# Banded attention feeding a two-layer MLP on one core: V's way to the windows, the mask and the first batch rearranged

## The chip, the cores and the metric

The kernel runs on one core of a Trainium2 chip. The metric is device time in microseconds, from the first to the last instruction of the program, as the median of several runs. The engines of the core are TensorE (PE in the profile, with its weight loads as PEld), VectorE (DVE), ScalarE (ACT), GpSimd (POOL) and SyncE (SP). SyncE and ScalarE start transfers through hardware queues, GpSimd through a software queue; all of them share 16 DMA engines.

## The reference

Eight batches with eight heads each, 576 positions, head size 64. Each position looks at itself and the 63 positions before it. The output of attention, 4608 rows of 512, goes through a two-layer network with 2048 hidden units.

```python
batch, n_heads, seq, head_dim = (8, 8, 576, 64)
n_tokens, d_model, d_ff = (4608, 512, 2048)

scores = np.matmul(q, k.transpose(0, 1, 3, 2)) / np.sqrt(D)
rel = pos[:, None] - pos[None, :]
mask = (rel >= 0) & (rel < 64)
attn = softmax(np.where(mask, scores, -1e9))
x = (attn @ v).transpose(0, 2, 1, 3).reshape(B * S, H * D)
h = x @ w_in
g = h - np.tanh(h)
return g @ w_out
```

## The kernel before

**Attention.** The 576 positions of a batch are nine windows of 64 queries. A window of queries sees 128 keys: its own 64 and the 64 before. Heads are worked in pairs (NP = 4 pairs in a batch, 32 pairs in all, numbered g). For a pair the kernel needs kT and qT (head dimension on the partitions), computes scores with keys on the partitions, takes the exponential on ScalarE into PT, and multiplies PT with the V window `vw[b % 2]`, which holds for each window j the 128 keys on its partitions, all heads, and a column of ones that gives the denominators. `norm` divides on VectorE and writes xs, with queries on the partitions. xs is then turned to xT (features on the partitions): by `x_tr`, transposes on TensorE that are copied out of PSUM by two engines, or by `x_dma`, DMA transposes on SyncE's queue (L346).

**V.** `load_v` or `load_v_all` brings V through GpSimd's queue, which casts from float32 to bf16, to 72 partitions with eight positions each. `cast_v` rearranges it to `vb`, where a position has all its heads side by side. `keys_v` sends 64 keys from eight partitions of vb to the upper half of one window, one transfer for each of the nine windows. The lower half of window j + 1 is the upper half of window j: `shift_v` copies it, as one DMA of 64 partitions (L176) or as copies on VectorE (L174). The shift waits for all nine transfers that it reads. Lower and upper half of each window are in place only then. vb exists once, so the casts of the next batch wait for the transfers that read it.

**The mask.** Batches 0 and 1 (pairs 0 to 7) go through `tile_scores` and `tile_pv`, where an additional product with `hide` pushes forbidden scores far down. Pairs from 8 on go through `scores`, `masking` and `pv`; their mask is made on GpSimd as `seen` and turned by TensorE into PSUM (`make_mask`).

**The network.** Nine chunks of 512 tokens (c = 0 to 8). For each chunk 16 steps "h" (four products with w_in, L361, then tanh on ScalarE, L366, and a subtraction on VectorE, L373) and 16 steps "y" (four products with w_out, L385; after four such steps a copy on ScalarE to one of three ysb buffers and an output transfer on SyncE's queue).

**Order.** Everything is ordered by hand. Before the first step stands batch 0: loads, products that only keep TensorE busy (`warm`, L238), casts, transposes of k and q for a pair (`tr_heads`), scores, PV, norms and turns. Then come 320 numbered steps h; `OPS` says which product stands at which step: chunk 0's h at the even steps 0 to 30, its y at 32 to 47, chunk 1's h at 48 to 63, its y at 64 to 79, chunk 2's h at 80 to 95, and from step 96 on h of chunk c at the even steps and y of chunk c - 1 at the odd ones. `at(h, ...)` hangs attention work behind the product of step h. Each engine works through its own queue in the order in which the program emits it, so an instruction that waits holds all behind it on that engine. `std` hangs the parts of one pair: casts, transposes (`tr`, bank 3), scores (bank 4), masking, PV and norm. In the loop over pairs from 12 on, a is the step of a pair's first transpose, cv the step of a V cast, ky that of the V transfers, sh that of the shift. GpSimd holds back some loads by `pace`, a one-element copy that waits for a certain step of the network.

The lines of the steps that matter most in the version before:

```python
at(36, lambda: [cast_v(1, pr, V) for pr in range(NP)])
at(37, lambda: [keys_v(1, j, G) for j in range(NJ)])
at(38, make_mask)
at(49, lambda: [keys_v(2, j, G) for j in range(NJ)])
at(58, shift_v, 2, 0, NJ - 1, Y)
```

Of the kernel before, what the change touches and what calls it, by code (L numbers as in the profile page):

```python
# [15 lines left out]
def kernel(  # L16
# [27 lines left out]
    qk_pool = ctx.enter_context(tc.tile_pool(name="qk", bufs=3))  # L44
# [36 lines left out]
    def move(eng, o, i):  # L81
        if eng is nc.scalar:
            nc.scalar.activation(o, i, ACT.Copy)  # L83
        else:
            eng.tensor_copy(o, i)  # L85

    def load(g, n, eng):

        b, pr = divmod(g, NP)
        if eng is nc.gpsimd:  # L90
            if (b, n) not in whole:
                whole[b, n] = all_pool.tile([P, H, E * D], BF16, tag=n, name=n + "all")
            t = whole[b, n][:, pr::NP]
        else:
            t = qk_pool.tile([P, 2, E * D], F32, tag="f", name=n + "f")
        eng.dma_start(out=t, in_=(q if n == "q" else k)[b, pr::NP].rearrange("h (p e) d -> p h (e d)", e=E))
        stage[g, n] = t
# [18 lines left out]

    def cast_flat(g, n, eng):
        t = row_pool.tile([P, E, 2, D], BF16, tag=n + "b", name=n + "b").rearrange("p e h d -> p (e h d)")
        t = t.rearrange("p (h c) -> p h c", h=2)
        move(eng, t, stage.pop((g, n)))  # L120
        stage[g, n] = t
# [27 lines left out]
    def load_v(b, pr):  # L149
        if (b, "v") not in whole:  # L150
            whole[b, "v"] = v_pool.tile([PV, H, EV * D], BF16, tag="v", name="vall")
        t = whole[b, "v"][:, pr::NP]
        nc.gpsimd.dma_start(out=t, in_=v[b, pr::NP].rearrange("h (p e) d -> p h (e d)", e=EV))
        stage[b, pr, "v"] = t

    def load_v_all(b):
        t = v_pool.tile([PV, H, EV * D], BF16, tag="v", name="vall")
        nc.gpsimd.dma_start(out=t, in_=v[b].rearrange("h (p e) d -> p h (e d)", e=EV))
        for pr in range(NP):
            stage[b, pr, "v"] = t[:, pr::NP]  # L160

# [41 lines left out]

    nc.vector.memset(ident, 0.0)
    nc.vector.memset(hide, 0.0)
    nc.vector.memset(qT[0], 0.0)
    for i in range(2):
        nc.vector.memset(kT[i][:, 0:64], 0.0)
    nc.vector.memset(vb[:, :, :, D], 1.0)
# [8 lines left out]

    def make_mask():
        nc.gpsimd.memset(seen, 1.0)  # L220
        nc.gpsimd.affine_select(seen, seen, compare_op=ALU.is_ge, fill=0.0,
                                base=-1, pattern=[[1, 128]], channel_multiplier=-1)
        nc.gpsimd.affine_select(seen, seen, compare_op=ALU.is_ge, fill=0.0,
                                base=64, pattern=[[-1, 128]], channel_multiplier=1)
        nc.tensor.transpose(mask, seen, ident[0:64, 0:64])
# [9 lines left out]
    def warm(n):  # L235

        for _ in range(n):
            nc.tensor.matmul(ps[:, 7, :], qT[0][:, 0, 0:128], qT[0][:, 0, 0:512], start=True, stop=True)  # L238

    def tr_heads(g, which, bank, eng):  # L240

        src = stage.pop((g, which))
        tp = ps[:, bank, :].bitcast(BF16)[:, 0:E * P].rearrange("c (e p) -> c e p", e=E)
        for e in range(E):
            for h in range(2):
                nc.tensor.transpose(tp[64 * h:64 * h + 64, e, :], src[:, h, D * e:D * e + D], ident[:P, :P])  # L246
        o = qs[g % 2] if which == "q" else kT[g % NR][:, 64:]
        move(eng, o.rearrange("c (p e) -> c p e", e=E), tp.rearrange("c e p -> c p e"))
# [103 lines left out]
    gT = {}  # L352
# [55 lines left out]
    def at(h, fn, *args):  # L408
        items.setdefault(h, []).append((fn, args))
# [12 lines left out]
    load(0, "q", Y)  # L422
    load(0, "k", A)
    for pr in range(NP):
        load_v(0, pr)
# [4 lines left out]
    for g in 2, 3:  # L430
        load(g, "k", G)
        load(g, "q", G)

    warm(8)
    cast_flat(0, "q", V)
    cast_flat(0, "k", A)
    tr_heads(0, "k", 2, V)
    tr_heads(0, "q", 3, A)
    for pr in range(NP):
        cast_v(0, pr, V)  # L440
    tile_scores(0, 0, (0, 1))
    tile_scores(0, 1, (4, 5))
    for j, eng in enumerate((Y, G, A, Y, G, G, A, Y, G)):
        keys_v(0, j, eng)
    load_w_in(0)
    load_w_in(1)
    for g, eq in (1, A), (2, V), (3, V):
        tr_heads(g, "k", 2, V)
        tr_heads(g, "q", 3, eq)
        tile_scores(g, 0, (0, 1))  # L450
        tile_scores(g, 1, (4, 5))
# [6 lines left out]
    load(7, "k", G)  # L458
    shift_dve(0, 0, 4)
    tile_pv(0, (6, 7))  # L460
    tile_pv(1, (2, 3))
    x_tr(0, 0, 0, 4, 4, A)
    tile_pv(2, (6, 7))
    x_tr(0, 0, 4, 9, 5, A)
    warm(3)
    tile_pv(3, (2, 3))
    warm(3)
# [3 lines left out]
    at(34, more_constants)  # L471
    at(36, lambda: [cast_v(1, pr, V) for pr in range(NP)])
    at(37, lambda: [keys_v(1, j, G) for j in range(NJ)])
    at(37, load, 7, "q", G)
    at(37, load_v_all, 2)
    for g in 8, 9:
        at(37, load, g, "k", G)
        at(37, load, g, "q", G)
    at(38, make_mask)
# [3 lines left out]
    at(41, tr_heads, 5, "k", 3, V)  # L483
    at(42, tr_heads, 5, "q", 0, A)
    at(42, tile_scores, 4, 1, (4, 5))
    at(43, tile_scores, 5, 0, (4, 5))
    at(43, tr_heads, 6, "k", 3, V)
    at(44, tr_heads, 6, "q", 0, A)
    at(44, tile_scores, 5, 1, (4, 5))
    at(45, tile_scores, 6, 0, (4, 5))  # L490
    at(45, shift_dve, 1, 0, 4)
    at(46, tr_heads, 7, "k", 3, V)
    at(46, tr_heads, 7, "q", 0, A)
    at(46, tile_scores, 6, 1, (4, 5))
# [12 lines left out]
    at(49, lambda: [keys_v(2, j, G) for j in range(NJ)])  # L507
# [3 lines left out]
    at(58, shift_v, 2, 0, NJ - 1, Y)  # L511
# [30 lines left out]
    for g in range(3 * NP, B * NP):  # L542
# [3 lines left out]
        cv, ky, sh = s - 72 + 5 * pr, s - 54, s - 47  # L546
        if b == 3:
            a = (65, 71, 76, 81)[pr]
            cv, ky, sh = 63 + pr, 67, 73
        elif b == 4:  # L550
            a = 84 + 7 * pr
            cv, ky, sh = 74 + 3 * pr, 86, 92
        elif b == 5:
            cv, ky, sh = 95 + 4 * pr, 110, 116
        at(cv, cast_v, b, pr)
        if b == 3:
            std(g, a - 1, a - 2, a, a + 2, a + 3, a + 8, a + 11)
            if pr == 0:
                for j in range(NJ):
                    at(ky + j // 2, keys_v, b, j)  # L560
                at(sh, shift_v, b, 0, NJ - 1)
            if pr == NP - 1:
                at(a + 12, x_dma, b)
            continue
# [22 lines left out]
        for j in range(NJ):  # L587
            if pr == 0:
                at(ky + j // 2, keys_v, b, j)
        if pr == 0:  # L590
            if b > 3:
                hq, hk = s - (60 if b < 7 else 68), s - (64 if b < 7 else 72)
                hv = {4: 69, 5: 92}.get(b, s - 78)
                if b == 4:
                    hq, hk = 72, 71
                for h, f in (hv, (load_v_all, b)), (hq, (load_all, b, "q")), (hk, (load_all, b, "k")):
                    at(h, pace, h)
                    at(h, *f)
            at(sh, shift_v, b, 0, NJ - 1)
# [52 lines left out]
```

## Time and profile before

| | |
|---|---|
| median of 3 runs | 391.17 us |
| lowest, highest | 386.18, 395.22 us |
| span of the profiled run | 389.9 us |
| mean granted TensorE clock | 0.950 |
| TensorE busy | 335.6 us, 86% |
| VectorE busy | 197.7 us, 51% |
| ScalarE busy | 182.1 us, 47% |
| GpSimd busy | 115.8 us, 30% |
| first product of chunk 0 | at 31.1 us |

The page divides the span into 40 slices of 9.75 us; each digit is the busy share of a slice in tenths. In the row of TensorE, 9 is full and a low digit is a gap:

```profile
PE   7869938978887699259969999999699999999996
DVE  4345801358834568407853766666266644344310
PEclk9999976999999899759996999999899999999999
DMA  9999768569398132991367759945971130101012
```

TensorE has two deep gaps, in the sixth slice (48.8 to 58.5 us) and in slice 17 and 18 (156 to 175 us). The granted clock is lower in and behind them. A group of instructions is listed with its busy time, the mean duration of one, and the idle time of its engine before it, with what ended that idle time. The two groups of the network's products on TensorE are the two largest:

```profile
L361 PE MATMUL ps<-xT,wi 128*128 128x512 bf16 x576 | 147.2, 384 | 15.6 <-DMA xT<-xs 10.4
L385 PE MATMUL ps<-w_out_sb,gT 128*128 128x512 bf16 x576 | 148.7, 389 | 0.0
```

### The profile page before, as it was taken

To read this page: it belongs to the slowest core of one execution; us is meant where nothing else is said; L and a number is where in the kernel's file an instruction comes from. 1 tells how busy PE (TensorE), PEld (TensorE's weight loads), DVE (VectorE), ACT (ScalarE), POOL (GpSimd) and SP (SyncE) were. 2 spreads that over 40 slices of the span, in tenths; PEclk is the share of its full clock that TensorE was granted. 3 is DMA by queue.
4 is the path that set the end of the run, shared out by engine and by line. 5 is a ranking of instruction groups with operands and counts; after the bars stand their busy time and mean duration, and the time that the engine had idled before them with its cause. 6 is when DMAs were issued, how large, how long until landed. Compare 5 with 4: busy or idle time off the path is not lost.

```text
span 389.9 us, 6205 instructions
## 1 busy us (share of the span) xinstructions
PE 335.6 (86%) x2421; PEld 180.1 (46%) x2421; DVE 197.7 (51%) x317; ACT 182.1 (47%) x329; POOL 115.8 (30%) x171
## 2 busy tenths in 40 slices
PE   7869938978887699259969999999699999999996
PEld 3544513545544455035534555555255544444442
DVE  4345801358834568407853766666266644344310
ACT  3324502557744287216643766665255434434421
POOL 8801084972632900262133332381000000000000
PEclk9999976999999899759996999999899999999999
DMA  9999768569398132991367759945971130101012
GB/s 161 182 212 205 117 108 145 103 94 191 45 128 199 41 84 61 103 139 46 59 131 128 137 116 165 158 107 134 201 183 55 50 93 29 54 27 49 33 55 82
DMA packets 51486, 42.98 MB, mean 110 GB/s; under 512 B 23328, under 2 KB 44576, under 8 KB 51072
## 3 DMA queue, kind: packets, MB, share of 16 engines
q0 software_dynamic: 21488, 19.54, 33.6%
q1 hardware_dynamic: 29616, 22.62, 23.5%
q10 hardware_dynamic: 352, 0.43, 0.4%
q8 instruction: 19, 0.31, 0.3%
q14 instruction: 11, 0.09, 0.1%
HBM read 36.70 MB, written 11.21 MB: 123 GB/s over the span
## 4 chain that ended last, share of the span: by engine, by line
PE 59%; DMA 14%; DVE 10%; POOL 6%; issue 6%; ACT 4%; SPq 1%; POOLq 0%; ACTq 0%; DVEq 0%
PE ps L385 26%; PE ps L361 23%; DMA vw<-vb 6%; DVE gT L373 3%; DMA xT<-xs 3%; DMA vw<-vw 3%; PE ps L314 2%; PE ps L302 2%; DVE xs L325 2%; DMA vall<-in_v_dram 1%; POOL vw L168 1%; PE ps L254 1%; DVE xs L296 1%; DVE qt L85 1%; ACT th L366 1%
## 5 line engine op out<-in xcount | busy, mean ns | idle before, releaser
L361 PE MATMUL ps<-xT,wi 128*128 128x512 bf16 x576 | 147.2, 384 | 15.6 <-DMA xT<-xs 10.4
L373 DVE TENSOR_TENSOR gT<-ps,th 128x512 bf16<-128x512 f32 x144 | 98.2, 690 | 100.7 <-ACT th L366 98.8
L385 PE MATMUL ps<-w_out_sb,gT 128*128 128x512 bf16 x576 | 148.7, 389 | 0.0
L366 ACT ACTIVATE th<-ps 128x512 f32<-128x512 f32 x144 | 85.7, 598 | 89.5 <-PE ps L361 87.6
L361 PEld LDWEIGHTS <-wi 128*128 128x128 bf16 x576 | 62.1, 114 | 64.9 <-DMA xT<-xs 10.8
L385 PEld LDWEIGHTS <-gT 128*128 128x128 bf16 x576 | 54.3, 100 | 56.5 <-issue 3.8
L304 ACT ACTIVATE pt<-ps 128x384 bf16<-128x384 f32 x72 | 35.2, 489 | 45.8 <-PE ps L302 45.7
L85 POOL COPY vb<-vall 72x1024 bf16<-72x1024 bf16 x24 | 24.9, 1054 | 44.6 <-DMA vw<-vb 22.7
L325 DVE TENSOR_TENSOR xs<-ps,rc 64x576 bf16<-64x576 f32 x48 | 36.2, 755 | 1.2
L390 ACT ACTIVATE ysb<-ps 128x512 f32<-128x512 f32 x36 | 21.6, 599 | 31.3 <-PE ps L385 31.3
L314 PE MATMUL ps<-vw,pt 128*128 128x130 bf16 x216 | 23.2, 229 | 7.7 <-DMA vw<-vw 4.8
L302 PE MATMUL ps<-qt,kt 128*128 128x128 bf16 x216 | 24.6, 224 | 5.6 <-DMA kt<-kd 3.1
L314 PEld LDWEIGHTS <-pt 128*128 128x128 bf16 x216 | 17.7, 103 | 23.1 <-DMA vw<-vw 8.8
L302 PEld LDWEIGHTS <-kt 128*128 128x128 bf16 x216 | 17.1, 101 | 16.4 <-issue 4.2
L85 DVE COPY qt<-ps 64x576 bf16<-64x576 bf16 x20 | 15.2, 760 | 14.6 <-ACT qt L83 14.5
L85 DVE COPY kt<-ps 128x576 bf16<-128x576 bf16 x8 | 6.1, 758 | 29.6 <-PE ps L246 29.6
L85 POOL COPY qb<-qall 96x768 bf16<-96x768 bf16 x18 | 14.9, 828 | 18.9 <-DMA qall<-in_q_dram 11.7
L308 DVE TENSOR_TENSOR pt<-pt,ps 128x1152 bf16<-128x1152 bf16 x24 | 17.9, 746 | 1.4 <-ACT pt L304 1.4
L85 POOL COPY kb<-kall 96x768 bf16<-96x768 bf16 x22 | 18.1, 832 | 0.0
L168 POOL DMA_DIRECT2D vw<-vb x22 | 13.0, 609 | 10.3 <-DVE vb L85 10.0
L280 ACT ACTIVATE pt<-ps 128x640 bf16<-128x640 f32 (+1 forms) x16 | 10.4, 650 | 10.3 <-PE ps L277 10.3
L414 POOL COPY tick<-gT 1x1 bf16<-1x1 bf16 x12 | 2.2, 181 | 43.8 <-DVE gT L373 43.8
(68 smaller groups left out, 206.6 us busy)
## 6 DMA issues: line engine op xcount, KB each, us to landing
out_dram<-ysb SPq DMA_DIRECT2D x36, 256.0 KB
vall<-in_v_dram POOLq DMA_DIRECT2D x7, 576.0 KB, 9.0
vw<-vb SPq DMA_DIRECT2D x48, 65.0 KB
vw<-vw SPq DMA_DIRECT2D x6, 520.0 KB
kall<-in_k_dram POOLq DMA_DIRECT2D x4, 576.0 KB, 9.2
qall<-in_q_dram POOLq DMA_DIRECT2D x4, 576.0 KB, 7.9
kall<-in_k_dram POOLq DMA_DIRECT2D x15, 144.0 KB, 8.8
qall<-in_q_dram POOLq DMA_DIRECT2D x15, 144.0 KB, 8.9
```

The source lines that it names most:

```text
L85: eng.tensor_copy(o, i)
L168: eng.dma_start(out=vw[b % 2][64:128, j].rearrange("p h c -> p (h c)"), in_=vb[8 * j:8 * j + 8].rearrange("p e h c -> p e (h c)"))
L302: nc.tensor.matmul(sp[:, i, :], kT[g % NR][:, 64 * j:64 * j + 128], qT[g % NR][:, :, 64 * j:64 * j + 64], start=True, stop=True)
L304: nc.scalar.activation(PT[g % NPT][:, 3 * grp:3 * grp + 3, :], sp, ACT.Exp, scale=scale)
L308: nc.vector.tensor_tensor(p, p, mask.unsqueeze(1).to_broadcast([128, 2 * NJ, 64]), ALU.mult)
L314: nc.tensor.matmul(ps[:, 5 + grp, 130 * i:130 * i + 130], PT[g % NPT][:, j, :], vw[b % 2][:, j, 2 * pr:2 * pr + 2, :], start=True, stop=True)
L325: nc.vector.tensor_tensor(xo[r, :, :, pr, :], ov[r, :, :, h, 0:D], rc[r].to_broadcast([64, 3, 3, 64]), ALU.mult)
L361: nc.tensor.matmul(hp, w_in_tile(ki, m), chunk_tile(c)[:, :, ki % 2, 64 * (ki // 2):64 * (ki // 2) + 64], start=(ki == 0), stop=(ki == 3))
L366: nc.scalar.activation(th, hp, ACT.Tanh)
L373: nc.vector.tensor_tensor(gT[c][:, m, :], hp, th, ALU.subtract)
L385: nc.tensor.matmul(yp, gT[c][:, m, s * 128:(s + 1) * 128], w_out_sb[:, m, :], start=(m == 0), stop=(m == M - 1))
L390: nc.scalar.activation(ysb, ps[:, yp_bank(c, s), :], ACT.Copy)
```

## The change

Four things are done.

1. The mask `seen` is made at the beginning, by `make_seen` on GpSimd, and turned into PSUM at step 34 by `see`; before, both stood at step 38 behind the transfers and loads of step 37 in GpSimd's queue. It is to keep TensorE from waiting on GpSimd's queue.
2. From batch 2 on, V goes from vb to the windows as spans of 128 keys: `windows_v` sends for window 0 the upper half as before, and for each other window all 128 keys at once, read from 16 partitions of vb that overlap with those of the next span. The shift is gone there. The nine transfers of a batch stand at one step on SyncE's queue (batch 2: GpSimd's), from batch 6 on at five steps.
3. Batch 3 is turned by TensorE (`x_tr`) at steps 83, 84, 93 and 94 and no longer by DMA transposes.
4. The first batch is rearranged. V comes first, as float32, through the hardware queues (`load_v_wide`, into memory of a gT buffer), and is cast by VectorE (three pairs) and ScalarE (one). k and q of pair 0 come by GpSimd's queue as the others do. Thirteen idle products stand at first instead of eight, and the six later ones are gone. The transposes of the next pair stand ahead of scores and PV of the one before. V's transfers of batch 0 stand ahead of the loads of pair 3. The steps of some casts, loads and pairs are moved by one or two; in batch 4 the pairs begin two steps earlier.

```diff
+    def load_v_wide(pr, eng):
+        if (0, "v") not in whole:
+            whole[0, "v"] = g_pool.tile([128, M, TOK], BF16, tag="gT", name="v32").rearrange("p m t -> p (m t)").bitcast(F32)[
+                0:PV].rearrange("p (h c) -> p h c", h=H)
+        t = whole[0, "v"][:, pr::NP]
+        eng.dma_start(out=t, in_=v[0, pr::NP].rearrange("h (p e) d -> p h (e d)", e=EV))
+    def windows_v(b, j, eng):
+        if j == 0:
+            keys_v(b, 0, eng)
+        else:
+            eng.dma_start(out=vw[b % 2][:, j].rearrange("p h c -> p (h c)"),
+                          in_=vb[8 * j - 8:8 * j + 8].rearrange("p e h c -> p e (h c)"))
...
-    load(0, "q", Y)
-    load(0, "k", A)
     for pr in range(NP):
-        load_v(0, pr)
+        load_v_wide(pr, (Y, A)[pr % 2])
+    load(0, "k", G)
+    load(0, "q", G)
...
-    warm(8)
-    cast_flat(0, "q", V)
-    cast_flat(0, "k", A)
-    tr_heads(0, "k", 2, V)
-    tr_heads(0, "q", 3, A)
-    for pr in range(NP):
+    warm(13)
+    for pr in range(NP - 1):
         cast_v(0, pr, V)
-    tile_scores(0, 0, (0, 1))
-    tile_scores(0, 1, (4, 5))
-    for j, eng in enumerate((Y, G, A, Y, G, G, A, Y, G)):
+    cast_v(0, 3, A)
+    for j, eng in enumerate((Y, G, A, G, Y, A, G, Y, G)):
         keys_v(0, j, eng)
+    for n in "kq":
+        load(3, n, G)
...
+    tr_heads(1, "k", 2, V)
+    tr_heads(1, "q", 3, A)
+    tr_heads(2, "k", 2, V)
+    tile_scores(1, 0, (0, 1))
+    tile_scores(1, 1, (4, 5))
+    tr_heads(2, "q", 3, V)
     shift_dve(0, 0, 4)
     tile_pv(0, (6, 7))
-    tile_pv(1, (2, 3))
-    x_tr(0, 0, 0, 4, 4, A)
-    tile_pv(2, (6, 7))
-    x_tr(0, 0, 4, 9, 5, A)
-    warm(3)
-    tile_pv(3, (2, 3))
-    warm(3)
+    tr_heads(3, "k", 2, V)
+    tile_scores(2, 0, (0, 1))
+    tile_scores(2, 1, (4, 5))
+    tr_heads(3, "q", 3, A)
+    tile_pv(1, (6, 7))
+    tile_scores(3, 0, (0, 1))
+    tile_scores(3, 1, (4, 5))
+    x_tr(0, 0, 0, 4, 0, A)
+    x_tr(0, 0, 4, 9, 1, A)
+    tile_pv(2, (2, 3))
+    tile_pv(3, (6, 7))
     x_tr(0, 1, 0, 4, 4, V)
     x_tr(0, 1, 4, 9, 5, A)
...
-    at(37, lambda: [keys_v(1, j, G) for j in range(NJ)])
+    at(34, see)
+    at(35, lambda: [keys_v(1, j, G) for j in range(NJ)])
...
-    at(38, make_mask)
...
-    at(49, lambda: [keys_v(2, j, G) for j in range(NJ)])
+    at(49, lambda: [windows_v(2, j, G) for j in range(NJ)])
...
-    at(58, shift_v, 2, 0, NJ - 1, Y)
...
-            a = 84 + 7 * pr
-            cv, ky, sh = 74 + 3 * pr, 86, 92
+            a = 82 + 7 * pr
+            cv, ky = 74 + 3 * pr, 85
         elif b == 5:
-            cv, ky, sh = 95 + 4 * pr, 110, 116
+            cv, ky = 95 + 4 * pr, 108
...
                 for j in range(NJ):
-                    at(ky + j // 2, keys_v, b, j)
-                at(sh, shift_v, b, 0, NJ - 1)
-            if pr == NP - 1:
-                at(a + 12, x_dma, b)
+                    at(67, windows_v, b, j, Y)
+            if pr % 2:
+                at(a + 12, x_tr, b, pr // 2, 0, 4, 3, V)
+                at(a + 13, x_tr, b, pr // 2, 4, 9, 3, A)
...
-                at(ky + j // 2, keys_v, b, j)
+                at(ky + (j // 2 if b > 5 else 0), windows_v, b, j, Y)
...
-            at(sh, shift_v, b, 0, NJ - 1)
```

## What was predicted before the change ran

> **What bounds the kernel now.** I read first the busy time of each engine by stage, cut where TensorE (PE) stops or starts: microseconds, then busy time (and instructions) of PE, its weight loads, VectorE (DVE), ScalarE (ACT) and GpSimd (POOL), the granted clock, the DMA engines' busy share and GB/s.
>
> ```profile
> 1.65:31.10 29.45, 23.41 (x296) 13.01 (x297) 12.76 (x26) 9.63 (x15) 16.70 (x27) 1.00 1.09 197
> 31.10:51.90 20.80, 20.23 (x96) 9.92 (x93) 13.62 (x23) 10.76 (x19) 3.25 (x6) 1.00 0.83 146
> 51.90:60.02 8.12, 0.00 (x0) 0.00 (x1) 0.00 (x0) 0.00 (x0) 7.92 (x15) 0.64 0.82 118
> 60.02:83.10 23.08, 21.16 (x319) 11.16 (x320) 8.92 (x16) 9.34 (x16) 14.49 (x20) 0.90 0.70 117
> 83.10:159.40 76.30, 62.26 (x487) 36.76 (x484) 50.01 (x81) 45.42 (x90) 33.23 (x45) 0.98 0.57 103
> 159.40:169.70 10.30, 0.00 (x0) 0.00 (x0) 1.34 (x3) 0.59 (x1) 4.15 (x6) 0.53 1.25 154
> 169.70:202.20 32.50, 31.35 (x224) 17.53 (x225) 20.64 (x33) 18.79 (x36) 7.48 (x10) 0.94 0.41 78
> 202.20:280.00 77.80, 70.96 (x481) 39.37 (x481) 45.85 (x71) 42.61 (x77) 28.12 (x42) 0.95 0.76 142
> 280.00:388.00 108.00, 106.24 (x528) 52.38 (x526) 43.90 (x66) 44.60 (x77) 0.00 (x0) 0.99 0.23 67
> ```
>
> From 280 us on PE is full: 108 us that no rearrangement of attention shortens. Two stretches have no product in them, 8.12 and 10.30 us. The waits of PE name what ends them:
>
> ```profile
> PE ps L361 <- DMA xT<-xs: 10.4, 1, 10.4
> PE ps L225 <- POOL seen L223: 8.1, 1, 8.1
> PE ps L314 <- DMA vw<-vw: 4.8, 3, 3.2
> ```
>
> So: the DMA transposes of batch 3's attention output (L346), the causal mask that GpSimd makes, the DMA that shifts V's windows (L176). The chain of work that ended last has the third twice; start, length and what:
>
> ```profile
> 116.87 6.61 DMA vw<-vb
> 123.62 6.17 DMA vw<-vw
> 129.83 1.05 PE ps L314 x8
> ...
> 193.84 6.97 DMA vw<-vb
> 200.88 4.72 DMA vw<-vw
> 205.65 0.40 PE ps L314 x2
> 206.05 0.32 PE ps L302 x3
> 206.37 1.71 PE ps L361 x4
> ```
>
> The last line also shows what a gap leaves behind: four 512-column products take 1.71 us after it, 0.86 us in the steady stretch. In the timeline GpSimd issues nine V transfers from 49.92 for 5.07 us, then six loads, and only at 58.94 begins the mask (0.31, 0.28 and 0.28 us); that queue is what PE waits for.
>
> **What the Trainium skill says.** "TensorE: Matmul & The Clock Gate", Part 1: an idle array falls to 1.2 GHz and needs about 3.4 us of activity in a free-running window to return to 2.4. The trace agrees: the half-rate products run from 60.02 to about 64.45, from 169.71 to about 173.5, and from 205.65 to about 210.5. "DMA: Bandwidth & Descriptors", "Why a DMA increments its semaphore by 16 and not by 1": a transfer runs on the largest number of engines up to 16 that divides both sides' slowest dimension. By it today's V transfer (8 source partitions) would use 8 engines, a span of 128 keys (16 source partitions) 16, and the float32 load of V (72 partitions) 12; the trace does not show this count. The same page, "Issuing engines are not separate DMA queues": all queues interleave on the same 16 engines. The trace agrees: the DMA share is 1.09 over the first 29 us, with three queues at work.
>
> **The change, part by part.**
>
> *Mask ahead (make_seen at the start, its transpose at step 34).* GpSimd makes it while loads stream, some 0.6 us of its time near 5 us. It removes 8.15 us idle. The following half-rate stretch, 60.02 to 64.45, holds 4.43 us of work that takes half at full rate: 2.2 us more. V of batch 1 must still land before step 45: its issues end at 54.97 and a GpSimd V transfer lands in 3.5 us, so 58.5; without the stall PE gets to its PV products at about 65.6 (51.9, 2.2 for the two steps it did cold, 11.5 as from 64.45 to 76.0). Hidden. Gain 10.3.
>
> *Batch 3 turned by PE instead of DMA.* Removed: 10.36 us idle and about 1.9 us of half rate behind it. Added: 18 transposes (nine take 0.68 us at full rate): 1.4 us on PE; and four evictions, 0.42 us on DVE and 0.77 on ACT for each half. In this stage DVE is the busy engine (18.07 of 20 us from 140 to 160), so DVE's 0.84 us lie on the path. The transposes stand in PE's queue behind norm of pair 15, ending at 157.56, and share bank 3 with batch 4's transposes; behind them stand the last products of chunk 2. From 157.56: first transposes and copy 0.8, products and queue about 2, second transposes and ACT copy 1.2: chunk 3 starts near 162 instead of 169.7, a gain of 7.7. Plus 1.9 clock, minus 1.3 for the first half's transposes and their bank: 8.3.
>
> *V as spans of 128 keys (windows_v).* Nine transfers and one shift that waits for all nine become nine that wait for none. Batch 3: the chain 116.87 to 129.79 loses the 6.17; PE's idle there is 1.87 + 1.10 and it restarts cold: 3.0 taken. Batch 5: idle 1.00 + 3.23, then 4.9 us of half rate (2.4); PE may still wait the 1.00 for DVE: 5.4. Later batches: only 0.45 at 275.8. Each transfer now carries 130 KB instead of 65, so bytes are those of the nine and the shift together. The unknown is its landing: from 3.5 us as the small one on GpSimd's queue to 6.97 as the last small ones on SyncE's. Either is hidden: batch 5's would be issued after its casts (177 us), nine issues of 0.62 us, landed at 190 at the latest, wanted at 202. The waits are on SyncE's queue, with output transfers behind them; three ysb buffers stand between those and ACT.
>
> *First batch.* V now comes as float32 by the SyncE and ACT queues, 4 x 288 KB, ahead of k and q. Today the two 288 KB loads on these queues land at 5.05 and 5.35 us; twice the bytes, sharing with GpSimd's queue, give 7 to 9. Casts: 96x768 from float32 takes 0.61 us on DVE, 0.84 on ACT, so 72x1024 some 0.8 and 1.1; the last ends near 8.8, against 9.45 today. The copies of k and q stand behind the casts on DVE and ACT, so scores of pair 0 begin near 10.5, not 7.4. What follows is the chain 10.99 to 21.26, a V transfer on SyncE's queue among the weight loads; I take 9 to 10 us for it again, as the DMA engines stay full. Then PE still has two pairs' scores to do (3.5 us a pair today) beside PV, norms and turns, where today all scores are done and PE waits on norms. First product of chunk 0: 29.5 instead of 31.1, between 25 (w_in's first half lands at 24.93, whoever asks) and 32. Thirteen products at first, not eight (0.43 us each): 2.1 us under the loads, cost nothing; but warm(3) twice is gone, so chunk 0 may begin cold, up to 2 us. Net gain 1.5, from -2 to +6.
>
> *Slots of loads.* Issues of 0.63 to 0.86 us on GpSimd; k and q of pairs 4 to 7 land by 46.7, their use begins after 48. Nothing.
>
> *New waits.* PE comes to chunk 1 ten us sooner, GpSimd's queue and its loads do not: V of batch 3 lands at 90.7 and pair 12's q is cast after it, by 94.3, where PE would want it at about 94. With bank 3 I put 2 us there, from 0 to 12.
>
> Sum: 10.3 + 8.3 + 3.0 + 5.4 + 1.5 - 2 = 26.5; 391.2 - 26.5 = 364.7, taken as 364.
>
> **Rivals.**
>
> 1. *Everything clears* (0.15). Start 4 us better, no new wait: 364 - 4 - 2 - 3 = 355. For it: PE's busy time after the start is 335.6 - 23.4 = 312.2; less 6.5 for the three half-rate stretches, plus 1.4 for turns, 307; with 28 for the start, some 15 of short waits and 4 at the end, 354. Against it: DVE's 90% in chunk 2 does not fall.
>
> 2. *The stalls are handed to GpSimd and the loads* (0.21). The chain takes GpSimd's row of casts and loads between 80 and 100 as its new leader; half of the mask's gain (5) and half of the turns' (4) come back as waits, and the start brings nothing (2): 364 + 11 = 375. For it: GpSimd is busy 14.49 of 23.08 us in that stage, and it waits for V's landing. Against: casts of pair 10 end at 82.4 and PE wants them near 87.
>
> 3. *Slower* (0.04). The windows' waits on SyncE hold back outputs, ysb runs out and ACT stops PE; with five batches (3 to 7) at 5.6 us, nine issues of 0.62, and a cold start (+3) the gain is gone: 364 + 28 + 3 = 395. Against: ScalarE is idle at least 40% in every stage and outputs are due every eight steps.
>
> **How the numbers follow.** Forecast 0.60, rivals 0.15, 0.21, 0.04. The predicted time is the forecast's, 364. The range runs from just under the first rival, 354, to just past the second, 376; the fourth case and a worse second lie outside, as does a little of the first. Faster by over 2% means under 383.3: all of forecast and first rival and nearly all of the second, 0.94; within 2%, 0.03; slower, 0.03.
>
> **What would show it.** Right: no PE wait on seen near 52; no xT<-xs DMA before chunk 3; no vw<-vw DMA at all; half-rate products only at the start. Start right if chunk 0's first L361 product comes between 27.5 and 31. New waits would read as PE L254 (transposes) behind POOL qb or kb between 75 and 100. Wrong, if PE shows a new idle stretch over 5 us after 31, or if out_dram transfers bunch up behind vw<-vb on SyncE.

## The result, and the profile after

The changed kernel takes 363.93 us (median of four runs, 361.24 to 367.27) against 390.88 us for the kernel before in the same comparison: a ratio of 0.9325, 95% interval 0.9199 to 0.945. The profiled run has a span of 359.5 us (361.24 in the metric) and is the fastest of its runs; the profile of before (span 389.9) is near the median. So the stages below differ by 30.4 us in sum, and the medians by 27. Totals are taken from medians here and stages from profiles.

The same table of busy time by engine, cut at the marks that answer to those of before:

```profile
1.60:30.40 28.80, 19.73 (x295) 11.84 (x296) 12.01 (x25) 10.66 (x16) 15.56 (x26) 0.70 1.02 191
30.40:51.10 20.70, 20.10 (x96) 10.02 (x94) 13.62 (x23) 10.74 (x19) 3.81 (x7) 1.00 0.96 169
51.10:71.75 20.65, 18.10 (x317) 10.81 (x318) 8.84 (x16) 9.44 (x16) 13.66 (x21) 1.00 0.80 131
71.75:130.00 58.25, 47.17 (x371) 27.56 (x372) 34.29 (x57) 34.35 (x67) 36.61 (x50) 0.97 0.74 131
...
153.40:195.00 41.60, 40.52 (x311) 23.61 (x313) 29.38 (x46) 26.48 (x50) 18.72 (x24) 1.00 0.60 107
195.00:255.00 60.00, 58.53 (x405) 33.25 (x411) 39.94 (x62) 36.69 (x67) 19.90 (x30) 1.00 0.80 153
255.00:357.50 102.50, 99.96 (x489) 49.42 (x496) 40.79 (x61) 42.41 (x72) 0.00 (x0) 1.00 0.21 65
```

Neither of the two stretches without a product is left: chunk 0's y and the next batch's attention follow one another at 51.1 us with no gap of a microsecond. (31 of the 576 records of L385 are missing from this trace, so PE's busy time is a little low.) From 153 us on PE is busy over 97% of the time. The waits of PE that were the longest before (10.4 us for xT<-xs, 8.1 for seen, 4.8 for vw<-vw) are gone. These are now the longest:

```profile
PE ps L246 <- DMA kall<-in_k_dram: 3.5, 1, 3.5
PE ps L331 <- DVE xs L296: 3.5, 3, 1.9
PE ps L361 <- DVE gT L373: 3.1, 6, 1.5
PE ps L314 <- DVE xs L325: 1.9, 1, 1.9
PE ps L331 <- DVE qt L84: 1.8, 1, 1.8
PE ps L290 <- DVE vw L172: 1.8, 2, 1.6
PE ps L254 <- POOL kb L84: 1.7, 1, 1.7
```

The chain that ended last says the same in shares, first before, then after:

```profile
PE 59%; DMA 14%; DVE 10%; POOL 6%; issue 6%; ACT 4%; SPq 1%; POOLq 0%; ACTq 0%; DVEq 0%
PE 74%; DVE 8%; DMA 7%; ACT 5%; issue 2%; POOL 2%; ACTq 1%; SPq 0%; DVEq 0%; POOLq 0%
```

For the experiments it is handiest to cut a profile at the first product with w_in of each chunk (L361 in the two kernels). The table has the start of chunk 0 and then the time from one chunk's first product to the next one's, in us, read from each kernel's trace; the last column is the median of its runs, beside the kernel before on the same chip (389.9 to 390.9). The ratios leave out slow runs, those at a lower granted clock or over 1.5% above the fastest of their kernel, and for the same reason the spans alone stand in the table with their second run, p_win2 (the profile of the first, p_win, has a clock of 0.55 throughout).

| kernel | chunk 0 at | 0 to 1 | 1 to 2 | 2 to 3 | 3 to 4 | 4 to 5 | 5 to 6 | rest | median |
|---|---|---|---|---|---|---|---|---|---|
| before | 31.15 | 51.97 | 53.26 | 33.33 | 45.34 | 33.80 | 38.00 | 103.03 | 390.9 |
| changed | 30.41 | 41.34 | 51.52 | 29.14 | 36.25 | 33.80 | 33.46 | 103.58 | 363.9 |
| p_mask | 32.61 | 41.77 | 57.12 | 33.48 | 45.16 | 33.80 | 37.23 | 103.04 | 385.3 |
| m_win3 | 32.40 | 41.78 | 50.38 | 33.43 | 42.93 | 33.80 | 37.33 | 103.09 | 375.8 |
| p_win2 | 32.26 | 51.91 | 50.39 | 33.18 | 38.96 | 33.80 | 34.17 | 103.45 | 383.3 |
| p_turn | 32.27 | 53.11 | 51.00 | 29.17 | 42.26 | 33.81 | 33.50 | 103.58 | 382.7 |
| p_start | 31.48 | 53.19 | 50.99 | 30.52 | 43.49 | 33.80 | 37.85 | 103.39 | 386.2 |
| c_fill | 32.07 | 50.43 | 51.15 | 33.23 | 42.05 | 33.81 | 36.21 | 103.03 | 384.6 |
| n_win | 31.35 | 42.76 | 55.89 | 28.00 | 41.19 | 33.80 | 34.47 | 103.10 | 372.3 |
| n_V | 29.86 | 41.33 | 51.67 | 30.42 | 36.25 | 33.80 | 33.93 | 103.20 | 362.2 |
| x_bank | 30.81 | 41.33 | 51.53 | 27.56 | 36.25 | 33.80 | 33.61 | 103.39 | 360.8 |
| best1 | 30.00 | 42.44 | 50.75 | 29.28 | 36.25 | 33.80 | 34.44 | 103.45 | 359.5 |
| best2 | 30.62 | 42.61 | 50.38 | 29.07 | 36.25 | 33.80 | 36.54 | 103.07 | 360.3 |

One profile stands behind each row, and rows that are alike in a stage show how far it moves by itself. Batch 3's shift is the same in before, p_turn, p_start and c_fill, yet chunk 1 to 2 takes 53.3 us in the first and 51.0 to 51.2 in the others: in before, a clock record of half rate, 3.4 us long, begins at 129.3 while PE waits for the shift, and in the others there is none. From 0 to 1, p_turn and p_start are 1.1 and 1.2 us longer than before with the same stall. Differences of 1 to 2 us between two rows are therefore not shown to belong to an edit, unless the trace names the wait.

### The profile page after: what moved, and what is told of

Read it like the earlier page. It is cut to its first block, busy times and chain, and to the rows that moved or that the text cites. A ratio compares the mean times of both kernels' runs of the same rounds, so it can differ in the third digit from the quotient of the medians.

```text
span 359.5 us, 6211 instructions
## 1 busy us (share of the span) xinstructions
PE 322.7 (90%) x2407; PEld 178.0 (50%) x2438; DVE 196.3 (55%) x317; ACT 184.8 (51%) x334; POOL 113.5 (32%) x168
## 4 chain that ended last, share of the span: by engine, by line
PE 74%; DVE 8%; DMA 7%; ACT 5%; issue 2%; POOL 2%; ACTq 1%; SPq 0%; DVEq 0%; POOLq 0%
PE ps L385 33%; PE ps L361 28%; DMA qall<-in_q_dram 4%; PE ps L314 3%; PE ps L302 3%; DMA v<-in_v_dram 2%; PE ps L254 2%; DVE xs L325 2%; DVE gT L373 2%; PE ps L246 2%; PE ps L271 1%; ACT th L366 1%; PE ps L277 1%; DVE xs L296 1%; PE ps L331 1%
## 5 line engine op out<-in xcount | busy, mean ns | idle before, releaser
L361 PE MATMUL ps<-xT,wi 128*128 128x512 bf16 x576 | 145.1, 381 | 3.8 <-DVE gT L373 3.1
L385 PE MATMUL ps<-w_out_sb,gT 128*128 128x512 bf16 x545 | 139.6, 382 | 2.4 <-issue 0.8
L361 PEld LDWEIGHTS <-wi 128*128 128x128 bf16 x576 | 61.7, 113 | 51.1 <-issue 5.6
L385 PEld LDWEIGHTS <-gT 128*128 128x128 bf16 x576 | 53.7, 98 | 56.2 <-issue 2.0
L314 PEld LDWEIGHTS <-pt 128*128 128x128 bf16 x216 | 16.7, 98 | 15.3 <-issue 2.0
L314 PE MATMUL ps<-vw,pt 128*128 128x130 bf16 x216 | 21.4, 220 | 2.3 <-DVE xs L325 1.9
L280 ACT ACTIVATE pt<-ps 128x640 bf16<-128x640 f32 (+1 forms) x16 | 10.3, 650 | 13.9 <-PE ps L277 13.9
L92 POOL DMA_DIRECT2D kall<-in_k_dram x16 | 11.2, 702 | 11.0 <-DMA wi<-in_moe_w_in_dram 5.4
L82 ACT ACTIVATE kt<-ps 128x576 bf16<-128x576 bf16 x20 | 13.0, 648 | 2.0 <-PE ps L254 1.9
```

The source lines that it names most:

```text
L314: nc.tensor.matmul(ps[:, 5 + grp, 130 * i:130 * i + 130], PT[g % NPT][:, j, :], vw[b % 2][:, j, 2 * pr:2 * pr + 2, :], start=True, stop=True)
L361: nc.tensor.matmul(hp, w_in_tile(ki, m), chunk_tile(c)[:, :, ki % 2, 64 * (ki // 2):64 * (ki // 2) + 64], start=(ki == 0), stop=(ki == 3))
L385: nc.tensor.matmul(yp, gT[c][:, m, s * 128:(s + 1) * 128], w_out_sb[:, m, :], start=(m == 0), stop=(m == M - 1))
```

## Experiments

### The mask ahead, alone (p_mask)

```diff
+    nc.vector.memset(seen, 1.0)
...
     make_hide()
+    make_seen()
...
+    at(34, see)
...
-    at(38, make_mask)
```

> The kernel before with the mask ahead alone. Theory (idle time and half-rate stretch both go, GpSimd's row has slack): 10.3 us faster, 380.6; the stage from chunk 0's first product to chunk 1's falls from 52.0 to about 41.5 us, the others stay. Rival (the stall is handed to GpSimd and its loads): half of it returns in the stage from chunk 1 to chunk 2, 386.

Measured: 385.31 us, ratio 0.9843 (0.9763 to 0.9924), nearer the rival's 386 than the theory's 380.6. The stage of the stall loses 10.2 us, the predicted 10.3. But the next stage grows by 3.9, and the trace says where. PE at the PV products of batch 3, first in before (two lines), then in p_mask:

```profile
128.51 0.22 PE L314 MATMUL ps<-vw,pt 128*128 128x130 bf16 x1 [1.87 <-DVE xs L325]
129.83 1.05 PE L314 MATMUL ps<-vw,pt 128*128 128x130 bf16 x8 [1.10 <-DMA vw<-vw]
119.20 0.22 PE L316 MATMUL ps<-vw,pt 128*128 128x130 bf16 x1 [1.87 <-DVE xs L327]
124.93 1.05 PE L316 MATMUL ps<-vw,pt 128*128 128x130 bf16 x8 [5.51 <-DMA vw<-vw]
```

The wait of 5.51 us in the last bracket is the one that was 1.10 in the kernel before. PE came 9.3 us sooner, and the shift of V landed only 4.9 us sooner. The rival was right in good part: GpSimd's last cast of batch 3's V ended at 102.6 us in before and at 102.2 in p_mask, so V's first transfers left hardly sooner although PE was far ahead, and the shift still stood behind them. The next experiment takes away the shift and leaves GpSimd's row as it is.

### The mask, and spans for batch 3 only (m_win3)

```diff
 # p_mask, and
-                    at(ky + j // 2, keys_v, b, j)
-                at(sh, shift_v, b, 0, NJ - 1)
+                    at(67, windows_v, b, j, Y)
```

> The mask ahead, and spans of 128 keys for batch 3 alone. With the mask alone 3.9 of its 10.2 us came back between chunk 1 and chunk 2, where TensorE waited on the shift of batch 3. If that shift took them, this stage falls from 57.1 to about 51.5, total some 5.5 us under the mask alone (385.3): 379.8. If GpSimd's row of casts and loads took them: 57 again, 385.

Measured: 375.81 us, 0.9636 (0.9576 to 0.9695). The stage from chunk 1 to 2 is 50.4 instead of 57.1. With the shift of this one batch gone the mask keeps its 10 us, though GpSimd's casts of V end at 100.55, little sooner: the shift was the link that cost the time. The total fell by more than expected, 9.5 us under p_mask; 6.7 of it is this stage, and 2.2 the stage from chunk 3 to 4, where PE's wait on batch 5's shift is 2.1 instead of 3.1 us in this profile and the half-rate record behind it 3.4 instead of 6.8. The edit does not touch that shift.

### The spans alone (p_win, p_win2)

```diff
+    def windows_v(b, j, eng):
...
-    at(58, shift_v, 2, 0, NJ - 1, Y)
...
-                at(ky + j // 2, keys_v, b, j)
+                at(ky + (j // 2 if b > 5 else 0), windows_v, b, j, Y)
...
-            at(sh, shift_v, b, 0, NJ - 1)
```

> The kernel before with the spans of 128 keys alone (batches 2 to 7). As predicted (batch 3: 3.0, batch 5: 5.4, later nothing): 382.5. By the stages of the changed kernel (chunk 1 to 2: 1.7, chunk 3 to 4: 7.2, chunk 5 to 6: 4.5, all of them owed to the spans): 377.5. Rival (transfers of 130 KB hold up others on SyncE's queue): no gain in chunk 5 to 6.

Measured: 386.36 us, 0.9819 (0.9707 to 0.993), nearer the 382.5 of the prediction than 377.5. For its stages the kernel was run a second time.

> The kernel before with the spans of 128 keys alone, run again for a profile at the full clock. If the spans' worth before the other parts is that of the waits on shifts in the profile before: chunk 1 to 2 from 53.3 to about 51, chunk 3 to 4 from 45.3 to about 38 (36.3, and 1.9 us of half rate behind the transposes' stall, which stays), chunk 5 to 6 anywhere from 34 to 38; total 381 to 383.

Measured: 383.33 us, 0.9749 (0.9678 to 0.9821). Chunk 1 to 2 gains 2.9 us and chunk 3 to 4 gains 6.4; they were predicted at 3.0 and 5.4. Chunk 5 to 6 gains 3.8, where the prediction had 0.45. All this is against the one profile of before. Against p_turn, p_start and c_fill, which keep the shift, chunk 1 to 2 gains only 0.6 to 0.8 us; and chunk 3 to 4 takes 42.1 to 45.2 us in other kernels that keep the DMA transposes and batch 5's shift, so the gain there is 3.1 to 6.4 us. In the medians the whole is 7.6, and 3.6 in the first run of the same kernel: the spans alone are worth less than their profile says.

### All but the spans (n_win)

```diff
 # the changed kernel, with
-    at(49, lambda: [windows_v(2, j, G) for j in range(NJ)])
+    at(49, lambda: [keys_v(2, j, G) for j in range(NJ)])
+    at(58, shift_v, 2, 0, NJ - 1, Y)
...
-                    at(67, windows_v, b, j, Y)
+                    at(ky + j // 2, keys_v, b, j)
+                at(sh, shift_v, b, 0, NJ - 1)
```

> The changed kernel with V's windows as before (64 keys and a shift, at the old steps), all else changed. If the spans are what lets the mask's gain through (with the mask alone the stage from chunk 1 to 2 grew from 53.3 to 57.1 us, with PE waiting on the shift of batch 3): that stage is again 56 to 57, against 51.5; chunk 3 to 4 is 42 to 45 against 36.3; 375 to 377 in all. Rival (spans worth only what the prediction summed, 8.4 minus the new wait of 2): 370. Chunk 5 to 6 stays at 33.5 if the turns and not the spans made it short (it was 33.5 with the turns alone).

Measured: 372.29 us, 0.9562 (0.9484 to 0.964), between the two expectations. The stages are close to what the first one said: 55.9 and 41.2 us, against 51.5 and 36.3 with the spans, and PE again waits 7.8 us in three places on vw<-vw. With these waits part of the mask's gain is lost again, and this is the plainest evidence for the spans: in the medians they are worth 8.4 us here, and the two intervals do not overlap. Chunk 5 to 6 is 34.5, near the 33.5 with the spans: that stage is not theirs alone.

### Batch 3 turned by TensorE, alone (p_turn)

```diff
-            if pr == NP - 1:
-                at(a + 12, x_dma, b)
+            if pr % 2:
+                at(a + 12, x_tr, b, pr // 2, 0, 4, 3, V)
+                at(a + 13, x_tr, b, pr // 2, 4, 9, 3, A)
```

> The kernel before with batch 3 turned by TensorE alone; batch 4 keeps its steps. As predicted: 8.3 us faster, 382.6. By the stages of the changed kernel (chunk 2 to 3: 4.2, and 1.9 us of half rate behind it): 384.8. If the two steps by which batch 4 was moved cost chunk 2 its gain, this kernel has the whole 8.3.

Measured: 382.74 us, 0.9788 (0.9712 to 0.9864). Chunk 2 to 3 loses 4.2 us and chunk 3 to 4 another 3.1: 7.2 in sum, against 8.3. Of the 3.1, 2.0 are the half rate behind the old stall, which lasted from 169.71 to 173.71 us in before and is gone; the other 1.15 are a shorter wait on batch 5's shift, 2.08 instead of 3.23, which this edit does not touch. In chunk 2 to 3 PE meets waits that the sum did not have, two of 2.12 us for norm on VectorE and one of 0.92 for bank 3:

```profile
143.29 0.40 PE L331 MATMUL ps<-ident,xs 128*128 128x128 bf16 x4 [2.12 <-DVE xs L325]
147.02 0.42 PE L254 MATMUL ps<-ident,qb 96*128 96x96 bf16 x6 [0.92 <-ACT xT L83]
160.48 0.40 PE L331 MATMUL ps<-ident,xs 128*128 128x128 bf16 x4 [2.12 <-DVE xs L325]
```

Batch 4 keeps its steps here and chunk 2 to 3 is 29.2 as in the changed kernel (29.1), so moving batch 4 by two steps shows no loss there.

### The turns in other banks (x_bank)

```diff
 # the changed kernel, with
-                at(a + 12, x_tr, b, pr // 2, 0, 4, 3, V)
-                at(a + 13, x_tr, b, pr // 2, 4, 9, 3, A)
+                at(a + 12, x_tr, b, pr // 2, 0, 4, 6, V)
+                at(a + 13, x_tr, b, pr // 2, 4, 9, 7, A)
```

> The changed kernel with batch 3's turns in banks 6 and 7, free after norm, instead of bank 3, which they share with the transposes of batch 4. If the shared bank is what cost the turns half their predicted gain (waits of 1.80, 0.83 and 0.23 us near 131 to 136, and a half-rate window behind): the stage from chunk 2 to 3 falls from 29.1 to 26 or 27. If VectorE's load sets that stage: 29 again.

Measured: 360.75 us, 0.9268 (0.9204 to 0.9331); chunk 2 to 3 is 27.6, between the two. In the changed kernel these two lines of PE's timeline show bank 3 being handed round, a turn behind a copy of q and a k behind a turn's copy:

```profile
130.94 0.50 PE L331 MATMUL ps<-ident,xs 128*128 128x128 bf16 x4 [1.80 <-DVE qt L84]
135.74 0.41 PE L254 MATMUL ps<-ident,kb 96*128 96x96 bf16 x6 [0.83 <-ACT xT L82]
```

With banks 6 and 7 these two waits are gone, and two others stand in their place, on GpSimd's cast of q for batch 4 and on norm:

```profile
127.73 0.43 PE L254 MATMUL ps<-ident,qb 96*128 96x96 bf16 x6 [1.76 <-POOL qb L84]
132.16 0.40 PE L331 MATMUL ps<-ident,xs 128*128 128x128 bf16 x4 [1.13 <-DVE xs L325]
```

The stage from chunk 2 to 3, in the changed kernel, in x_bank and in n_win, whose turns use bank 3 (length, PE busy, granted clock, DMA):

```profile
123.27:152.41 29.14, 22.89 (x179) 0.94 0.67 108
123.67:151.23 27.56, 21.28 (x178) 1.00 0.67 104
130.00:158.00 28.00, 21.29 (x179) 1.00 0.66 111
```

PE is idle for 6.25 us in the first and 6.28 in the second: other banks took no idle time away. What is gone is the half-rate record of 3.4 us at 131.1, and that does not go with the bank: n_win has none with bank 3, and best1 and best2 below have one at 127.8 and 128.8 with banks 6 and 7 (29.3 and 29.1 us). So it is not shown that the shared bank cost the turns their gain. PE waits here for banks, for norm and for GpSimd's casts, and with the waits on the bank away the other two took their time.

### Idle products in the mask's stall (c_fill)

```diff
 # the kernel before, with
+    at(38, warm, 37)
     at(38, make_mask)
```

> The kernel before with 37 idle products (8.0 us at full rate) put ahead of the mask's transpose, where TensorE stands still for 8.15 us; the stall for the mask itself stays. If half rate behind the gap costs what the prediction took (2.2 us): chunk 0's first product to chunk 1's falls from 52.0 to 49.8, total 388.5. If the slow products there have another cause: 52.0 again, or longer by what the idle products overrun.

Measured: 384.55 us, 0.9859 (0.9754 to 0.9963). PE's timeline over the stall, first three lines of before, then c_fill:

```profile
60.02 0.23 PE L225 MATMUL ps<-ident,seen 64*128 64x64 bf16 x1 [8.15 <-POOL seen L223]
60.19 1.89 PE L385 MATMUL ps<-w_out_sb,gT 128*128 128x512 bf16 x4
62.01 0.69 PE L246 MATMUL ps<-ident,kall 96*64 96x96 bf16 x12
53.11 8.15 PE L238 MATMUL ps<-qt 128*128 128x512 bf16 x36
61.38 0.20 PE L225 MATMUL ps<-ident,seen 64*128 64x64 bf16 x1
61.52 1.04 PE L385 MATMUL ps<-w_out_sb,gT 128*128 128x512 bf16 x4
62.48 0.45 PE L246 MATMUL ps<-ident,kall 96*64 96x96 bf16 x12
```

Four products behind the stall take 1.04 us, where they took 1.89 before; twelve transposes take 0.45 instead of 0.69. The stage is 1.5 us shorter than that of before, although its own first 0.9 us (to 33.0) are at half rate, which those of before are not; with that, about 2.0, near the 2.2 of the prediction. It is 2.7 shorter than that of p_turn and p_start (53.1 and 53.2), which also begin chunk 0 at half rate. The cost of the cold clock behind a gap is real and separate from the gap.

### The first batch alone (p_start), and with its old loads (n_V)

```diff
 # p_start: the kernel before, with the new first batch
-    load(0, "q", Y)
-    load(0, "k", A)
     for pr in range(NP):
-        load_v(0, pr)
+        load_v_wide(pr, (Y, A)[pr % 2])
+    load(0, "k", G)
+    load(0, "q", G)
...
 # n_V: the changed kernel, with
+    load(0, "q", Y)
+    load(0, "k", A)
     for pr in range(NP):
-        load_v_wide(pr, (Y, A)[pr % 2])
-    load(0, "k", G)
-    load(0, "q", G)
+        load_v(0, pr)
```

> The kernel before with the new first batch alone (V as float32 by the hardware queues, new order, thirteen idle products). As predicted: chunk 0's first product 1.5 us earlier, 389.4. By the changed kernel's trace: 0.7 us earlier, 390.2. Neither is clear of the spread of the runs; the mark in the profile decides.

Measured: 386.18 us, 0.9888 (0.9823 to 0.9954). Chunk 0 begins at 31.48. In the six profiles of kernels that have the old start it begins between 31.15 and 32.61 (32.1 in the mean), in the four with the new one between 30.41 and 31.48 (31.0), so the whole new start is worth about 1 us at that mark. It can be lost behind the mark: p_start and n_win begin chunk 0 at half rate, and their stage from 0 to 1 is 1.2 and 1.4 us longer than in before and in the changed kernel.

The total fell by 3.7. The profile does not put the rest at the start. Chunk 1 to 2 is 2.3 us shorter, as in p_turn and c_fill with the old start. The DMA transposes of batch 3 are 2.8 shorter: PE waited 7.5 there instead of 10.4. In that run GpSimd's 576 KB load of V was issued at 21.23 us after chunk 2's first product, 0.03 us behind the first transpose; in the profile of before at 19.81, 1.4 us ahead of it. Issuing the two transposes took 4.9 us and 8.4 us. Four other kernels (p_mask, m_win3, p_win2, c_fill) issue the load 1.4 us ahead, as before does, and wait 10.2 to 10.5 us. That the order of the two transfers makes the difference rests on this one case.

> The changed kernel with the first batch's loads as before (q and k of pair 0 as float32 by the hardware queues, V through GpSimd's queue with its cast), in the new order of work. Theory (the last float32 V load lands at 9.45 and its cast ends at 10.54, a us later than the old way, so the loads lose what the order wins): V's transfers leave at 9.5 instead of 10.6, chunk 0's first product at 29.4 instead of 30.4, total 363. Rival (V by hardware queues is what lets the new order pay): chunk 0 begins at 31 to 32.

Measured: 362.22 us, 0.9308 (0.9247 to 0.9369). V's transfers leave at 9.39 and chunk 0 begins at 29.86, 0.55 before the changed kernel. In the changed kernel the last of V's four float32 loads and what follows is this, in the timeline:

```profile
9.45 1.09 ACT L82 ACTIVATE vb<-v 72x1024 bf16<-72x1024 f32 x1 [6.33 <-DMA v<-in_v_dram]
10.56 3.48 SPq L166 DMA_DIRECT2D vw<-vb  x3
```

The cast on ScalarE had waited 6.33 us and starts at 9.45, where in the kernel before all casts were done. With the old loads chunk 0 begins at 29.86 (n_V), 30.00 and 30.62 (best1, best2), with the new ones at 30.41 to 31.48. So V by the hardware queues brought nothing that shows; what the new start gains comes from the rest of it, its order, its idle products and the place of V's transfers, which were not told apart.

### Candidates to beat both (best1, best2)

```diff
 # best1: x_bank and n_V, and
     cast_flat(0, "k", A)
+    tr_heads(0, "k", 2, V)
+    tr_heads(0, "q", 3, A)
+    tile_scores(0, 0, (0, 1))
+    tile_scores(0, 1, (4, 5))
     for pr in range(NP):
         cast_v(0, pr, V)
...
-    tr_heads(2, "q", 3, V)
     shift_dve(0, 0, 4)
+    tr_heads(2, "q", 3, A)
 # best2: best1, and warm(4) behind the scores of pair 0 and of pair 1, warm(6) ahead of the first PV
```

> A candidate to beat both: the changed kernel with batch 3's turns in banks 6 and 7, the first batch's loads as before, pair 0's transposes and scores ahead of the V casts in the queues of VectorE and ScalarE, and the copies of the shift ahead of pair 2's q. From the runs with one of them: 1.6 us from the bank, 0.55 from the loads, and pair 0's scores at 7.4 instead of 12: 359 to 360. If V's transfers of batch 0 set the start, the early scores bring nothing: 361.

> As best1, with 4, 4 and 6 further idle products in the gaps of the first batch. If they hold the full clock until V's transfers land (the changed kernel has 17 us of half rate from 8.2 on), the first batch's work after the landing takes 3 us instead of 5: 357.5. If the clock falls all the same, or the products are in the way: 360 or more.

Measured: best1 359.52 us, 0.9212 (0.9161 to 0.9264); best2 360.28 us, 0.921 (0.9157 to 0.9263). Both are below the two kernels in the medians, best1 below the changed kernel by 4.4 us, of which x_bank alone has 3.2; its interval overlaps with that of the changed kernel (0.9199 to 0.945), so it is not shown to be faster than that one. Early scores brought nothing: chunk 0 begins at 30.00. It also begins at half rate, until 32.2 (33.2 in best2), so chunk 1 begins at 72.4 and 73.2, later than the 71.2 of n_V. From chunk 2 to 3 both wait for GpSimd's cast of q, 2.87 and 2.63 us. In best1 VectorE has nothing else to do when it comes to the two shifts of the first batch:

```profile
17.33 0.70 DVE L181 COPY vw<-vw 64x2080 bf16<-64x2080 bf16 x1 [4.46 <-DMA vw<-vb]
19.13 0.70 DVE L181 COPY vw<-vw 64x2080 bf16<-64x2080 bf16 x1 [1.09 <-DMA vw<-vb]
```

They wait for V's transfers, 65 KB each, the last of them until 9.8 us after the first had left at 9.36, among the loads of k, q and the weights. In best1 that sets the start. In the changed kernel it does not: there the shifts begin at 19.59 without such a wait, right behind VectorE's copy of q for pair 2. The two limits lie close together, so taking away one alone gains little. The further idle products shorten the half-rate stretch (13.7 us in best1, 6.8 in best2) and chunk 0 still begins at 30.62.

## Why the prediction was right

- *The mask: 10.3 predicted, 10.6 in the stage (10.2 alone).* The two terms, idle and half rate, are each shown: from before to p_mask PE's idle time in the stage falls by 8.15 us and its busy time by 2.05, and c_fill takes away the second and leaves the first. The sum had no term for what PE meets next, which took 3.9 us back in p_mask.
- *The turns: 8.3 predicted, 7.2 measured alone.* The half-rate term was right (2.0 where 1.9 stood). The stage's own gain was smaller (4.2 where 6.4 stood), since the two waits of 2.12 us behind norm in p_turn were not in the sum. The remaining 1.15 came from batch 5's shift, by no step of the prediction.
- *The spans: batch 3, 3.0 predicted and 2.9 found; batch 5, 5.4 and 6.4.* The agreement for batch 3 owes something to the profile of before: kernels with the same shift and no half-rate record behind it gain 0.6 to 0.8 us. The spans of batch 3 are worth 6.7 us once the mask is ahead (p_mask against m_win3), and the prediction had no such term.
- *Later batches: only 0.45.* This step failed. Chunk 5 to 6 is 4.5 us shorter in the changed kernel, 3.8 with the spans alone, and 4.5 with the turns alone, where the shift is still there. PE in before (two lines), in the changed kernel and in c_fill, each time with what it had waited for:

```profile
275.80 0.29 PE L314 MATMUL ps<-vw,pt 128*128 128x130 bf16 x2 [0.45 <-DMA vw<-vw]
279.14 0.34 PE L302 MATMUL ps<-qt,kt 128*128 128x128 bf16 x3 [3.06 <-DMA kt<-kd]
249.89 0.34 PE L302 MATMUL ps<-qt,kt 128*128 128x128 bf16 x3 [1.08 <-DMA kt<-kd]
271.24 0.34 PE L302 MATMUL ps<-qt,kt 128*128 128x128 bf16 x3 [1.82 <-DMA kt<-kd]
```

  In the kernel before, PE waits 3.06 us for batch 7's transposed k on SyncE's queue, and a half-rate record of 3.4 us follows at 279.5; in the changed kernel it waits 1.08 and no such record follows. The prediction did not name this wait. It is 3.1 to 3.3 us in p_mask, m_win3 and p_start, but 1.82 in c_fill, which has neither spans nor turns. So the gain of this stage is not shown to belong to either. Why the k comes sooner in so different kernels stays open; in p_turn batch 7's first q is cast 1.8 us sooner than in the kernel before, counted from chunk 5.
- *The first batch: 1.5 predicted, 0.7 against the profile of before, about 1 against the kernels with the old start.* The loads were mis-sized: V landed up to 9.45, not by 7 to 9, and its last cast ended at 10.54, not 8.8. The next term, 9 to 10 us for V's transfers, gave the right time by another path: the shifts began 9.0 us after the transfers had left, but behind VectorE's copies and not behind the transfers. The cold start that the prediction named came in p_start and n_win, not in the changed kernel.
- *New waits: 2 predicted.* In the stage where they were put none is shown. The wait that looks like it in the changed kernel is in the kernel before as well:

```profile
107.31 0.42 PE L254 MATMUL ps<-ident,qb 96*128 96x96 bf16 x6 [1.71 <-DVE qt L85]
95.17 0.41 PE L254 MATMUL ps<-ident,qb 96*128 96x96 bf16 x6 [1.72 <-POOL kb L84]
```

  In the changed kernel VectorE's copy of qt ends at 95.12 and GpSimd's kb at about the same time, and the profile names the later one. Chunk 1 to 2 is 1.1 us longer than with the spans alone for another reason: behind PE's wait of 1.87 us for norm stands a half-rate record at 117.4, and p_win2 has the wait without the record. A wait of PE on GpSimd's q came near 128 us: 0.27 us in the changed kernel, 1.76 in x_bank, 1.93 in n_V. In x_bank two clearings of the buffer `qz`, 1.38 us each, stand just ahead of that cast in GpSimd's queue; no run moved them.
- *The signs that were named.* No wait on seen, no DMA transposes before chunk 3, no shift by DMA, and chunk 0 at 30.41: as forecast. Half rate only at the start: not quite, for records of 3.4 us stand at 117.4 and 131.1.
- *The sum.* By stages the profiles differ by 30.4 us where the prediction had 26.5. Predicted and measured: the start 1.5 and 0.7, chunk 0 to 1 10.3 and 10.6, 1 to 2 1.0 (the spans' 3.0 less 2 for new waits) and 1.7, 2 to 3 6.4 and 4.2, 3 to 4 7.3 and 9.1, 5 to 6 nothing and 4.5; 0.5 went lost behind. By the ratios of the runs the parts alone are worth 1.6, 2.5 (1.8 in the first run), 2.1 and 1.1% of the time of before, 6.6 to 7.3 in all, against 6.75 together, each with an interval of 0.7 to 1.3 to either side: the totals cannot tell a plain sum from a coupled one. The stages can: of the mask's 10.2 us, 3.9 are lost without the spans of batch 3, and come back with them. The prediction summed the parts without that coupling; it did no harm since both were in.

That the forecast lies on the measured median is in part luck. The mechanism held for the two long stalls and the half rate behind them. Elsewhere misses of either sign nearly made up for each other, 4.5 us in chunk 5 to 6 were not foreseen, and 3.4 us of the profile's gain do not show in the medians.

## What to carry to other kernels

Price a stall of TensorE as its idle time plus the half-rate stretch behind it, and look at what the engine meets next if it comes ten us sooner: a wait of 1 us there can become one of 5, as the shift of V did. A transfer that waits for nine others and whose result PE needs at once is worth replacing even at the same number of bytes. Before moving a load to another queue, ask what comes behind it: here the transfers of V, in flight among other loads, and VectorE's copies set the start in turn, whatever queue the load of V took. And before giving a us or two to an edit, look whether a half-rate record stands in one of the two profiles and not in the other, and whether kernels that are alike in that stage differ by as much.

## What was not expected of the hardware

- The granted clock changes in steps: its half-rate records last 3.4, 6.8, 10.2 or 13.7 us, and 17.1 to 23.9 at the start of some runs, all multiples of 3.4. What a gap costs behind it is half of the time from its end to the end of the record: behind the mask's stall that time was 4.5 us in before, 5.8 in p_turn and 3.5 in p_start. Stages that end in a gap differ by that between kernels that are alike there: chunk 3 to 4 took 45.2 and 45.3 us in p_mask and before, with a record of 6.8 us behind the shift, and 42.1 to 43.5 in m_win3, c_fill and p_start, with one of 3.4 and a shorter wait.
- Small products with gaps between them did not bring the full clock here, and without gaps they did. In the changed kernel thirteen products of 512 columns brought it, and half rate returned at 8.2 us and stayed to 25.3. That stretch in pieces of 3.41 us (length, PE busy, granted clock, DMA):

```profile
8.19:11.60 3.41, 1.82 (x26) 0.50 1.10 168
11.60:15.01 3.41, 2.32 (x44) 0.50 0.92 148
15.01:18.43 3.42, 3.05 (x50) 0.50 0.99 162
18.43:21.84 3.41, 1.62 (x40) 0.50 1.08 190
21.84:25.25 3.41, 3.41 (x59) 0.50 1.12 207
25.25:28.67 3.42, 2.49 (x71) 1.00 1.13 216
```

  All five at half rate hold transposes, scores, mask products and PV products of 64 to 320 columns and none of 512. After four pieces that are 47 to 89% busy the clock stays low, and after the one that is busy throughout it rises. In p_mask a piece of such products that is 95% busy (11.83 to 15.25) was not enough either; in n_V and best1 the clock rose after a full one (to 24.84 and 25.40). With 512-column products in it, a piece that is 72% busy was enough (c_fill, 166.13 to 169.54). The Trainium skill, "TensorE: Matmul & The Clock Gate", Part 1, has the clock set by how busy the array was in a window of some 3.4 us and shows 128-column products lifting it when they come back to back. The trace agrees.
- The row PEclk of the kernel before shows 9 in its first three slices, while a 512-column product took 0.43 us there, twice the later time. The first clock record of that trace is at 30.35 us; durations of products are the safer reading.
